# Block 1's attention emitted directly after block 0's, and a first pass of four weight tiles instead of eight

## Chip, cores and metric

The kernel runs on one core of one Trainium2 chip. The metric is the device time of one execution in microseconds (us), the median of several executions. A profile is one execution more, taken with the hardware profiler on; its own time is given beside its span below.

## What is computed

Windowed causal attention over 8 batches, 8 heads, 576 positions and head size 64, and behind it a feed-forward layer with softplus on the 4608 tokens of width 512 (inner width 2048). All is float32.

```python
scores = scale * np.matmul(q, k.transpose(0, 1, 3, 2))
rel = pos[:, None] - pos[None, :]
mask = (rel >= 0) & (rel < window)          # window = 64
scores = np.where(mask, scores, -1000000000.0)
scores = scores - np.max(scores, axis=-1, keepdims=True)
attn = np.exp(scores)
attn = attn / (np.sum(attn, axis=-1, keepdims=True) + 1e-09)
x = np.matmul(attn, v)                      # then (tokens, heads * head size)
...
h = x @ w_in
g = np.maximum(h, 0.0) + np.log1p(np.exp(-np.abs(h)))
return (g @ w_out).astype(np.float32)
```

## The kernel before

The 4608 tokens are cut into 12 blocks of 384. For each block g the kernel runs the attention in four quarters (hp = 0 to 3, two heads each), which leave the attention's output x, transposed, as a high and a low part per quarter. Then come 16 steps, one per slice f of 128 inner columns. The first half of a step (`ffn_up`, L407) is 12 matmuls 128x384 that multiply x with slice f of w_in, three per quarter. Softplus follows on ScalarE (L411 to L413) and VectorE (L415); the result g is split into two parts (L417 on ScalarE, L418 on VectorE). The second half (`ffn_down`, L428) is 9 matmuls 128x512 that add g times slice f of w_out into three banks of the matmul accumulator. At the end of a block's steps the banks are copied out (L447) and stored (L448).

The weights arrive as 64-bit words, and `load_w(f)` makes float32 parts of slice f: a load by SyncE's queue (L168), one operation on ScalarE (L172), three on VectorE (L173 to L175), and for each of the two matrices a cast on ScalarE (L178) and a subtraction on VectorE (L179). For f up to 11 one load of 1024 KB fetches both matrices (tiles raws and ws); for f from 12 on it is two loads of 512 KB (raw and wh). The buffers of raw are two, and the stores of finished blocks use the same two.

Blocks 0 and 1 take a shorter form of the attention (by_pe): scores on TensorE (L260), the masked minimum on VectorE (L271, L277), the exponent on ScalarE (L281), the normalisation on VectorE (L286, L287, L289), transposes on TensorE (L296), copies back (L297), the product with v on TensorE (L353) and the split of x (L358 on ScalarE, L359 on VectorE). From block 2 on the operands are split into parts first (L238, L239, L244, L245), the scores are L264, and the transposes of the probabilities are made by DMA (L313, L318) ahead of the product with v (L382).

Block 0 goes over the weights in two passes. The first pass takes slices 0 to SPLIT-1, and its sums are stored in DRAM (L448, tile part). Then block 1 takes all 16 slices, and then block 0 takes the rest, and its first sums are fetched and added (L442). After that the blocks 2 to 11 follow. So the steps have one running number n: with SPLIT = 8 block 0 has n = 0 to 7, block 1 n = 8 to 23, block 0 again n = 24 to 31.

Each part of the work is an event with a number: `ffn_up` of step n stands at 2n + 0.5, `ffn_down` at 2n + DOWN, `load_w(f)` at CONVERT[f], and quarter hp of the attention of block g < 3 at BASE[g] + PACE[g] * hp plus the stage offsets of STG0 (or STG). The events are sorted and emitted in that order. That order sets priorities only: below PE_ORDERED_FROM = 100 the framework's scheduler orders the instructions of every engine, and from there on it orders all but TensorE. On each engine instructions run in the order that came out.

Of the kernel before, what the change touches and what calls it, by code (L numbers as in the profile page):

```python
# [20 lines left out]
CH = 64  # L21
NCH = TB // CH + 1

SPLIT = 8
DOWN = 5.5
CONVERT = (-95.5, -90.5, -85.5, -80.5, -6, -3, 0, 3, 6, 8, 11, 13, 16, 18, 21, 24)
BASE = (-100, -10, 24)
PACE = (5, 4, 7)
STG0 = (-4.5, 0.5, 1, 2, 3, 4, 7, 8)
STG = (-13, -5.9, -5, 0, 1, 2, 3, 4, 5, 6, 7, 7.1, 12, 14, 16, 17)  # L30
# [9 lines left out]
def window_attention_softplus_ffn(  # L40
# [111 lines left out]
    def load_w(f):  # L152


        if f < NE + 4:
            k = FIRST[f % 4] if f < NE else (4, 6)[f % 2]
            parts = [(spare(k, [P, 2, DM], w_words.dtype, "raws"), spare(k + 1, [P, 2, DM], F32, "ws"), 0, 2)]
        else:
            parts = [
                (  # L160
                    ff.tile([P, 1, DM], w_words.dtype, name="raw"),
                    att.tile([P, 1, DM], F32, name="wh", tag=("v_in", "v12")[m]),
                    m, m + 1,
                )
                for m in range(2)
            ]
        for raw, w, m0, m1 in parts:
            nc.sync.dma_start(raw, w_words[f][:, m0:m1, :])  # L168
            words = raw.bitcast(U32).rearrange("p m (n two) -> p two m n", two=2)
            low, high = words[:, 0, :, :], words[:, 1, :, :]  # L170
            wb = w.bitcast(U32)
            nc.scalar.activation(w, high.bitcast(F32), AF.Abs, scale=REBIAS)  # L172
            nc.vector.tensor_scalar(wb, wb, 3, None, ALU.logical_shift_left)  # L173
            nc.vector.scalar_tensor_tensor(wb, high, 0x80000000, wb, ALU.bitwise_and, ALU.bitwise_or)  # L174
            nc.vector.scalar_tensor_tensor(wb, low, 29, wb, ALU.logical_shift_right, ALU.bitwise_or)  # L175
            for m in range(m0, m1):
                hi, lo = [weight(m, i, f) for i in range(2)]
                nc.scalar.copy(hi, w[:, m - m0, :])  # L178
                nc.vector.tensor_tensor(lo, w[:, m - m0, :], hi.bitcast(F32), ALU.subtract)  # L179
# [273 lines left out]

    passes = [(0, 0, SPLIT), (1, 0, NF), (0, SPLIT, NF)] + [(g, 0, NF) for g in range(2, NB)]
    steps = [(g, f, f == f0, f == f1 - 1) for g, f0, f1 in passes for f in range(f0, f1)]
# [5 lines left out]
    for g in range(NB):  # L461
        for hp in range(NP):
            if g < 3:
                base = BASE[g] + PACE[g] * hp
            else:
# [5 lines left out]
    for n, (g, f, first, last) in enumerate(steps):  # L471
        if f == loaded:
            events.append((CONVERT[f], lambda f=f: load_w(f)))
            loaded += 1
# [54 lines left out]
```

## Time and profile before

| | |
|---|---|
| median of 3 executions | 1032.41 us (1032.14 to 1032.76) |
| profiled execution, its own time | 1035.78 us |
| its span | 1034.0 us |
| mean granted TensorE clock | 0.97 |
| VectorE (DVE) busy | 802.4 us, 78% |
| ScalarE (ACT) busy | 741.9 us, 72% |
| moved by DMA | 119.05 MB, 115 GB/s on average |

In the profile PE is TensorE, PEld its weight loads, DVE VectorE, ACT ScalarE, POOL GpSimd, SP SyncE, which issues the DMAs (SPq). A row of a timeline gives the start and the busy time in us, the engine, line and operation, the tiles, the count, and in brackets the idle time ahead of it with what ended it. Instructions on VectorE and ScalarE overlap a little, so the distance from one start to the next, about 0.1 us less than the busy time, is what one costs in a full queue.

### The profile page before, as it was taken

How to read it: one execution, taken by the hardware profiler on the slowest of the kernel's cores; microseconds unless marked ns; L12 is line 12 of the kernel's file. 1: busy time of each engine (PE TensorE's matmuls, PEld its weight loads, DVE VectorE, ACT ScalarE, POOL GpSimd, SP SyncE). 2: the span in 40 equal slices, each digit the busy share in tenths (PEclk: the TensorE clock that was granted, in tenths of full speed). 3: DMA queues.
4: the chain of work that ended last, by engine and by line, in shares of the span. 5: the costliest groups of instructions: out<-in, count | busy, mean ns of one | idle time of the engine just before them, and what ended most of it. 6: DMA issues, size and time to landing. Idle time of an engine off the chain costs nothing.

```text
span 1034.0 us, 16622 instructions
## 1 busy us (share of the span) xinstructions
PE 982.4 (95%) x5888; PEld 867.2 (84%) x5888; DVE 802.4 (78%) x1817; ACT 741.9 (72%) x1705; POOL 3.9 (0%) x14
## 2 busy tenths in 40 slices
PE   6669579999999999999999999999999999999998
PEld 3458369888888899899988989899899889989997
DVE  6899786587878878878878878887988887974332
ACT  3567477687778778778778778878877877865443
POOL 1000000000000000000000000000000000000000
PEclk9679789999999999999999999999999999999999
DMA  6774353256445546535534634634635645521000
GB/s 189 279 227 137 107 138 83 49 156 150 113 97 122 140 93 119 147 83 119 157 82 114 163 82 113 162 84 112 154 91 104 158 97 103 140 49 31 31 1 31
DMA packets 203155, 119.05 MB, mean 115 GB/s; under 512 B 130880, under 2 KB 195136, under 8 KB 201536
## 3 DMA queue, kind: packets, MB, share of 16 engines
q1 hardware_dynamic: 203072, 118.00, 45.5%
q8 instruction: 46, 0.75, 0.3%
q14 instruction: 37, 0.30, 0.1%
HBM read 76.28 MB, written 10.22 MB: 84 GB/s over the span
## 4 chain that ended last, share of the span: by engine, by line
PE 88%; DMA 4%; DVE 4%; ACT 2%; issue 1%; SPq 0%; ACTq 0%; DVEq 0%
PE ps_h L407 37%; PE ps_o L428 37%; PE ps_a L382 5%; PE ps_a L264 5%; DMA raws<-in_w_words_dram 1%; PE ps_a L260 1%; PE ps_a L353 1%; ACT st L281 1%; DVE ws L175 1%; DMA tr<-nat 1%; DMA part<-raw 0%; DVE w L179 0%; DVE st L271 0%; DMA v_in<-in_v_dram 0%; DVE ws L174 0%
## 5 line engine op out<-in xcount | busy, mean ns | idle before, releaser
L407 PE MATMUL ps_h<-x,w 128*128 128x384 f32 x2304 | 450.5, 343 | 21.5 <-DVE u L415 7.3
L407 PEld LDWEIGHTS ps_h<-x,w 128*128 128x128 f32 x2304 | 407.5, 191 | 37.5 <-ACT w L178 12.3
L428 PE MATMUL ps_o<-w,g 128*128 128x512 f32 x1728 | 438.5, 397 | 0.4 <-DVE g L418 0.4
L428 PEld LDWEIGHTS ps_o<-w,g 128*128 128x128 f32 x1728 | 319.7, 189 | 58.8 <-DVE g L418 0.8
L411 ACT ACTIVATE u<-ps_h 128x384 f32<-128x384 f32 x192 | 94.0, 489 | 135.6 <-PE ps_h L407 133.0
L415 DVE SCALAR_TENSOR_TENSOR u<-ps_h,u 128x384 f32<-128x384 f32 x192 | 106.3, 554 | 73.2 <-ACT u L413 72.0
L281 ACT ACTIVATE st<-st,mn 128x128 f32<-128x128 f32 x288 | 111.9, 390 | 16.3 <-DVE st L277 16.3
L418 DVE TENSOR_TENSOR g<-u,g 128x384 fp32r<-128x384 f32 x192 | 105.7, 551 | 11.0 <-ACT g L417 9.4
L271 DVE CUSTOM_DVE_ANT_0 st<-ps_a,mask 128x192 f32<-128x192 f32 x216 | 69.7, 351 | 51.9 <-PE ps_a L264 50.7
L412 ACT ACTIVATE u<-u 128x384 f32<-128x384 f32 x192 | 100.8, 526 | 3.4
L413 ACT ACTIVATE u<-u 128x384 f32<-128x384 f32 x192 | 100.1, 522 | 4.0
L264 PE MATMUL ps_a<-k,q_hl 128*128 128x192 f32 x480 | 77.1, 284 | 0.9 <-DVE q_hl L239 0.9
L382 PEld LDWEIGHTS <-v 128*128 128x128 bf16 x1088 | 56.1, 98 | 23.5 <-issue 23.1
L382 PE MATMUL ps_a<-tr,v 128*128 128x128 bf16 (+1 forms) x1088 | 70.7, 213 | 1.9 <-DMA tr<-nat 1.9
L264 PEld LDWEIGHTS ps_a<-k,q_hl 128*128 128x128 f32 x480 | 67.3, 194 | 4.8 <-DVE q_hl L239 1.3
L417 ACT CAST g<-u 128x384 fp32r<-128x384 f32 x112 | 56.9, 509 | 13.7 <-DVE u L415 13.0
L312 ACT CAST nat<-st 128x768 bf16<-128x768 f32 x40 | 33.2, 831 | 41.8 <-DVE st L310 41.7
L281 ACT ACTIVATION_READ_ACCUMULATOR st<-st,mn 128x1 f32 x288 | 54.0, 187 | 0.0
L387 ACT COPY xf<-ps_a 64x384 f32<-64x384 f32 x80 | 38.1, 476 | 21.5 <-PE ps_a L382 20.2
L388 DVE TENSOR_TENSOR xf<-ps_a,xf 64x384 f32<-64x384 f32 x80 | 43.8, 548 | 5.0 <-ACT xf L387 3.7
L289 DVE TENSOR_TENSOR st<-st,sm 128x768 f32<-128x768 f32 x48 | 45.9, 957 | 1.4
L331 DVE TENSOR_TENSOR v_in<-v_in,v 128x896 f32<-128x896 f32 x40 | 43.5, 1087 | 3.1 <-ACT v L330 2.9
(80 smaller groups left out, 814.6 us busy)
## 6 DMA issues: line engine op xcount, KB each, us to landing
k_in<-in_kT_dram SPq DMA_DIRECT2D x80, 224.0 KB, 3.9
v_in<-in_v_dram SPq DMA_DIRECT2D x80, 224.0 KB, 3.6
q_in<-in_qT_dram SPq DMA_DIRECT2D x84, 192.0 KB, 4.0
raws<-in_w_words_dram SPq DMA_DIRECT2D x12, 1024.0 KB, 5.6
out_dram<-raw SPq DMA_DIRECT2D x12, 512.0 KB, 2.8
raw<-in_w_words_dram SPq DMA_DIRECT2D x8, 512.0 KB, 4.3
out_dram<-raw SPq DMA_DIRECT2D x12, 256.0 KB, 2.6
v_t<-in_v_dram SPq DMA_DIRECT2D x16, 96.0 KB, 3.6
```

The costliest lines, as they stand in the source:

```text
L264: mm(spv[:, hh, :], q_hl[:, hh, js], part[:, hh, kc], start=(hh == 0 and i == 0), stop=(hh == 1 and i == 1), skip_group_check=True,)
L271: nc.vector.tensor_tensor_reduce(st[:, hh, j, :], spv[:, hh, :], m, QSCALE, 3.0e38, ALU.add, ALU.min, mn[:, hh, j : j + 1])
L281: nc.scalar.activation(sv[:, i, 0:P], sv[:, i, 0:P], AF.Exp, bias=mn[:, hh, j : j + 1], scale=-1.0, accum_out=sm[:, i : i + 1])
L382: mm(av[:, osl], (v13 if s else v12)[:, c, hh, :, :], src, start=(i == 0), stop=(i == len(passes) - 1), skip_group_check=True,)
L407: mm(hv, weight(0, a, f)[:, c * P : (c + 1) * P], x[b][c], start=(i_mm == 0), stop=(i_mm == 3 * NC - 1))
L411: nc.scalar.activation(u, hv, AF.Abs)
L412: nc.scalar.activation(u, u, AF.Exp, scale=-1.0)
L413: nc.scalar.activation(u, u, AF.Ln, bias=1.0)
L415: nc.vector.scalar_tensor_tensor(gf, hv, 0.0, u, ALU.max, ALU.add)
L417: (nc.scalar.copy if g < 2 or f % 2 else nc.vector.tensor_copy)(gt[0], gf)
L418: nc.vector.tensor_tensor(gt[1], gf, gt[0].bitcast(F32), ALU.subtract)
L428: mm(ops[g][j], gt[a][:, js], weight(1, b, f), start=(first and i == 0), stop=(last and i == 2),)
```

## The change

Three of the numbers that place the events change.

```diff
-SPLIT = 8
+SPLIT = 4
 DOWN = 5.5
-CONVERT = (-95.5, -90.5, -85.5, -80.5, -6, -3, 0, 3, 6, 8, 11, 13, 16, 18, 21, 24)
-BASE = (-100, -10, 24)
+CONVERT = (-95.5, -85.5, -72.5, -60.5, -4, -2, 0, 2, 4, 6, 8, 10, 12, 14, 16, 18)
+BASE = (-100, -79, 24)
 PACE = (5, 4, 7)
```

Block 0's first pass now has the steps n = 0 to 3, block 1 has n = 4 to 19, block 0's rest n = 20 to 31. Block 1's attention is emitted from -83.5 on, directly behind block 0's (which ends at -77), instead of from -14.5 on. Slices 1 to 3 are converted later in the emitted order, slices 4 to 15 stand closer together.

What the scheduler makes of it is shown at three places. The first is VectorE behind the end of block 0's first pass, which is the last g1 of that pass (g1_971 before, g1_819 after). Before the change; wh_1043 and wh_1045 are slice 13, pt_623 belongs to the third quarter of block 1's attention and st_659 to its fourth, raw_1099 takes the first sums:

```order
L418 TENSOR_TENSOR g1_971<-u_965,g0_970 128x384
L179 TENSOR_TENSOR w111_1002<-wh_986,w101_1001 128x512
L179 TENSOR_TENSOR w011_993<-wh_1043,w001_992 128x512
L297 COPY pt_623<-ps_a_629 128x384
L173 TENSOR_SCALAR wh_1045<-wh_1045 128x512
L271 ISA st_659,mn_660<-ps_a_662,mask_c_112 128x192
L271 ISA mn_660 128x1
L271 ISA st_659,mn_660<-ps_a_662,mask_c_112 128x192
L271 ISA mn_660 128x1
L447 COPY raw_1099<-ps_o0_716 128x512
L174 SCALAR_TENSOR_TENSOR wh_1045<-raw_1044,wh_1045 128x512
```

After the change; ws_832 is slice 10, ws_790 slice 9, sm_446 belongs to the second quarter of block 1's attention:

```order
L418 TENSOR_TENSOR g1_819<-u_813,g0_818 128x384
L173 TENSOR_SCALAR ws_832<-ws_832 128x1024
L447 COPY raw_922<-ps_o0_777 128x512
L174 SCALAR_TENSOR_TENSOR ws_832<-raws_831,ws_832 128x1024
L447 COPY raw_926<-ps_o2_779 128x512
L286 TENSOR_SCALAR sm_446<-sm_446 128x6
L175 SCALAR_TENSOR_TENSOR ws_832<-raws_831,ws_832 128x1024
L173 TENSOR_SCALAR ws_790<-ws_790 128x1024
L287 RECIPROCAL sm_446<-sm_446 128x6
L174 SCALAR_TENSOR_TENSOR ws_790<-raws_789,ws_790 128x1024
```

The first pass now ends when slices 9 to 15 and more than two quarters of block 1's attention are still to come; before, these were two and a half slices and less than two quarters.

The second place is TensorE at the last quarter of block 1's attention. Before (ps_h_1005 and ps_h_1063 are the steps n = 8 and 9, the first two of block 1):

```order
L296 MATMUL ps_a_747<-ident_115,st_659 128x128 x3
L296 MATMUL ps_a_752<-ident_115,st_659 128x128 x3
L353 MATMUL ps_a_838<-pt_746,v_t_101 64x64 x12
L407 MATMUL ps_h_1005<-x0_3_1_836,w00_85 128x384
L407 MATMUL ps_h_1063<-x0_3_1_836,w00_85 128x384
L407 MATMUL ps_h_1005<-x1_3_1_837,w00_85 128x384
L407 MATMUL ps_h_1005<-x0_3_1_836,w01_86 128x384
L407 MATMUL ps_h_1063<-x1_3_1_837,w00_85 128x384
L407 MATMUL ps_h_1063<-x0_3_1_836,w01_86 128x384
L264 MATMUL ps_a_1192<-k0_1085,q_hl_1060 128x192
```

After (ps_h_842 and ps_h_884 are n = 4 and 5, again the first two of block 1):

```order
L296 MATMUL ps_a_614<-ident_115,st_571 128x128 x3
L296 MATMUL ps_a_619<-ident_115,st_571 128x128 x3
L353 MATMUL ps_a_637<-pt_613,v_t_101 64x64 x12
L407 MATMUL ps_h_842<-x0_3_1_635,w00_85 128x384
L407 MATMUL ps_h_884<-x0_3_1_635,w00_85 128x384
L407 MATMUL ps_h_842<-x1_3_1_636,w00_85 128x384
L407 MATMUL ps_h_842<-x0_3_1_635,w01_86 128x384
L407 MATMUL ps_h_884<-x1_3_1_636,w00_85 128x384
L407 MATMUL ps_h_884<-x0_3_1_635,w01_86 128x384
L264 MATMUL ps_a_1210<-k0_1132,q_hl_1107 128x192
```

The order is the same, but four steps fewer stand ahead of it.

The third place is SyncE's queue from the store of block 0's first sums on. Before:

```order
L448 DMA part_1098<-raw_1099 128x2x512
L214 DMA q_in_884<-in_qT_dram 64x2x384 x2
L168 DMA raw_1128<-in_w_words_dram 128x512
L217 DMA k_in_1037<-in_kT_dram 64x2x448 x2
L448 DMA part_1098<-raw_1103 128x512
L168 DMA raw_1130<-in_w_words_dram 128x512
L168 DMA raw_1199<-in_w_words_dram 128x512
L168 DMA raw_1201<-in_w_words_dram 128x512
```

After:

```order
L448 DMA part_921<-raw_922 128x2x512
L448 DMA part_921<-raw_926 128x512
L168 DMA raw_929<-in_w_words_dram 128x512
L168 DMA raw_931<-in_w_words_dram 128x512
L168 DMA raws_873<-in_w_words_dram 128x1024
L228 DMA v_t_101<-in_v_dram 128x3x128
L228 DMA v_t_101<-in_v_dram 64x3x128 x2
L217 DMA k_in_907<-in_kT_dram 64x2x448 x2
L168 DMA raw_985<-in_w_words_dram 128x512
L168 DMA raw_987<-in_w_words_dram 128x512
L168 DMA raw_1034<-in_w_words_dram 128x512
```

Before, four half slices (14 and 15) follow the store in the two raw buffers; after, all eight (12 to 15) do, and slice 12's two loads, which before stood early in the queue, are among them.

## Prediction

> **What bounds the kernel now.** I read the page first: the engines' shares and the slices of the span.
>
> ```profile
> span 1034.0 us, 16622 instructions
> ...
> PE 982.4 (95%) x5888; PEld 867.2 (84%) x5888; DVE 802.4 (78%) x1817; ACT 741.9 (72%) x1705; POOL 3.9 (0%) x14
> ...
> PE   6669579999999999999999999999999999999998
> ...
> PEclk9679789999999999999999999999999999999999
> ```
>
> TensorE is full from about the seventh slice (26 us each) to the end. So nearly everything that this change can win or lose lies in the first 155 us, and the rest of the kernel only moves earlier or later. What fills TensorE's gaps there is read from the busy time by stretch (columns as named in the first line):
>
> ```profile
> core 0: us, PE busy (x) PEld busy (x) DVE busy (x) ACT busy (x) POOL busy (x), PEclk, DMA share, GB/s
> 20.00:138.71 118.71, 86.33 (x462) 67.69 (x460) 103.47 (x228) 73.76 (x177) 0.00 (x0) 0.78 0.58 187
> 138.71:154.55 15.84, 11.68 (x63) 9.76 (x63) 14.89 (x41) 12.84 (x40) 0.00 (x0) 0.98 0.56 137
> 154.55:233.94 79.39, 79.39 (x464) 70.74 (x464) 56.11 (x123) 59.46 (x134) 0.00 (x0) 0.98 0.40 97
> ```
>
> From 20 to 138.71 us VectorE is busy for 103.47 of 118.71 us and TensorE for 86.33 at a granted clock of 0.78; from 154.55 on TensorE has no gap until 233.94. The cut at 138.71 is the first softplus (L415) of block 1, step n = 8, and 154.55 is the start of the 13th `ffn_up`. So **the start is VectorE's** (conversion of weights, attention of two blocks), and TensorE does steps beside it as far as it has weights and x. The idle 15.24 us of VectorE in the first stretch, by group (count, busy us and mean ns, then idle us and releaser):
>
> ```profile
> L173 DVE TENSOR_SCALAR ws<-ws 128x1024 uint32<-128x1024 uint32 x12 | 8.2, 687 | 4.1 <-ACT ws L172 4.0
> L173 DVE TENSOR_SCALAR wh<-wh 128x512 uint32<-128x512 uint32 x8 | 3.4, 424 | 4.8 <-ACT wh L172 4.7
> L297 DVE COPY pt<-ps_a 128x384 f32<-128x384 f32 x5 | 2.8, 552 | 1.1 <-PE ps_a L296 1.1
> L286 DVE TENSOR_SCALAR sm<-sm 128x6 f32<-128x6 f32 x6 | 1.0, 161 | 4.1 <-ACT st L281 4.1
> ```
>
> 8.9 us wait for loaded weights, 4.1 us for the exponents of an attention quarter.
>
> **The change part by part.** Nothing is added or removed; the total work of every engine stays. A step moved from before block 1 to after it is what counts, because work beside VectorE's stage is covered and work behind it is not. The prices come from TensorE's timeline:
>
> ```profile
> 107.35 2.29 PE L407 MATMUL ps_h<-x,w 128*128 128x384 f32 x6 [3.38 <-DVE u L415]
> 109.44 2.76 PE L428 MATMUL ps_o<-w,g 128*128 128x512 f32 x6
> ...
> 139.31 2.36 PE L407 MATMUL ps_h<-x,w 128*128 128x384 f32 x12 [1.61 <-DVE u L415]
> ...
> 154.55 3.71 PE L407 MATMUL ps_h<-x,w 128*128 128x384 f32 x12 [2.02 <-DVE u L415]
> 158.09 2.24 PE L428 MATMUL ps_o<-w,g 128*128 128x512 f32 x9
> 160.17 2.27 PE L407 MATMUL ps_h<-x,w 128*128 128x384 f32 x12
> 162.28 2.25 PE L428 MATMUL ps_o<-w,g 128*128 128x512 f32 x9
> ...
> 231.23 0.59 PE L264 MATMUL ps_a<-k,q_hl 128*128 128x192 f32 x4
> 231.65 2.30 PE L407 MATMUL ps_h<-x,w 128*128 128x384 f32 x12
> 235.82 0.68 PE L382 MATMUL ps_a<-tr,v 128*128 128x64 bf16 x7 [1.88 <-DMA tr<-nat]
> 236.31 2.91 PE L428 MATMUL ps_o<-w,g 128*128 128x512 f32 x6
> 239.01 0.78 PE L264 MATMUL ps_a<-k,q_hl 128*128 128x192 f32 x4
> ```
>
> An `ffn_up` costs 162.28 - 160.17 = 2.11 us, an `ffn_down` 160.17 - 158.09 = 2.08, four scores of block 2 231.65 - 231.23 = 0.42.
>
> *VectorE's work ahead of block 1's first softplus.* Its row in VectorE's order has 271 instructions ahead of it before (20 to 138.71 shows x228, the first 20 us the rest) and 262 after. By kind the difference is: 4 of L415 and 4 of L418 fewer (the four steps), 2 of L271 with their 2 accumulator reads fewer, and one each of L174, L175 and L179 for a half slice more. The price of one is the distance to the next start:
>
> ```profile
> 135.46 0.68 DVE L179 TENSOR_TENSOR w<-wh,w 128x512 fp32r<-128x512 f32 x1
> 136.06 0.68 DVE L174 SCALAR_TENSOR_TENSOR wh<-raw,wh 128x512 uint32<-128x512 uint32 x1
> 136.66 0.35 DVE L271 CUSTOM_DVE_ANT_0 st<-ps_a,mask 128x192 f32<-128x192 f32 x1
> 136.94 0.08 DVE L271 DVE_READ_ACCUMULATOR2_ANT mn<- 128x1 f32 x1
> ...
> 138.71 0.55 DVE L415 SCALAR_TENSOR_TENSOR u<-ps_h,u 128x384 f32<-128x384 f32 x1
> 139.18 0.34 DVE L271 CUSTOM_DVE_ANT_0 st<-ps_a,mask 128x192 f32<-128x192 f32 x1
> ```
>
> That is 8 x 0.47 = 3.8 less, 2 x 0.28 = 0.6 less, 3 x 0.60 = 1.8 more: **2.5 us less** of 103.5. All slices but parts of the last, and all of block 1's attention, stand ahead of that softplus as before. Emitting block 1's attention at -83.5 does not bring its last x forward on VectorE: it is row 252 instead of row 256.
>
> *VectorE's idle time ahead of it.* Two causes shrink. Slice 12's two early half loads no longer stand ahead of slice 0, so slice 4's buffer comes free sooner, and most of the 4.1 us ahead of L173 (ws) should go: I take 2.5 to 3. And fewer steps stand in ScalarE's queue ahead of the exponents. One grows: slices 12 to 15 all pass the two raw buffers behind the store of block 0's first sums, where before it was 14 and 15. The chain of waits shows what one such passage is:
>
> ```profile
> 97.59 4.40 DMA k_in<-in_kT_dram
> 102.07 0.95 ACT k L244
> ...
> 120.92 4.99 DMA part<-raw
> 125.92 3.31 DMA raw<-in_w_words_dram
> 129.31 0.66 ACT wh L172
> ```
>
> Store 4.99, load 3.31, ScalarE 0.66. Of that VectorE has other work for a part, and two pairs more may bring 1 to 3 us more idle. The wait for k_in (4.40, then L244 0.95 ahead of the exponents on ScalarE) stays: k_in_907 still stands behind v_t_101 in SyncE's queue. From the order and these durations I get 3 us less idle in sum. The bounds: at best all four groups above go (14.1 us less), at worst two pairs more each pay store-free passages of 3.31 that nothing covers (6.6 us more). I take 3 less because the big items of both kinds stay. So block 1's first softplus comes at 138.71 - 2.5 - 3 = **133.2 us**, and TensorE's next `ffn_up` 0.6 us behind it, as 139.31 is behind 138.71: 133.8.
>
> *TensorE from there to the 13th `ffn_up`.* At that point both orders have 12 `ffn_up`, 10 `ffn_down` and 32 scores of block 2 behind them. Before, 2, 2 and 20 of these lie between 139.31 and 154.55: 4.2 + 4.2 + 5 x 0.42 = 10.5 us of work in 15.24, so 4.7 us of waiting and of lower clock. After, it is 6, 6 and 20: 12.7 + 12.5 + 2.1 = 27.3. The waits come from VectorE and ScalarE, which then do block 2's attention (VectorE 14.89 of 15.84 us busy). The same work now has four steps more to lie beside, and the conversions end earlier; I take half of the waits, 2.4, with 1 to 6 as bounds. That gives 133.8 + 27.3 + 2.4 = 163.5 against 154.55: **+9.0 us**.
>
> The lower clock after a wait is in these rows: 6 `ffn_up` matmuls behind the gap of 3.38 us took 109.44 - 107.35 = 2.09 us, twice 2.11 / 2. [...]
>
> *Behind it.* Before, the 13th `ffn_up` starts after a gap and takes 158.09 - 154.55 = 3.54 instead of 2.11; after, TensorE comes to it out of a full stretch: -1.4. The stall at 233.94 (1.88 us for the transposed probabilities, then six matmuls in 239.01 - 236.31 = 2.70 instead of 2.08 x 6 / 9 = 1.39) costs 3.2. There SyncE's queue holds block 1's output store and block 2's transposes close together; in the changed order the store stands four steps earlier and the last transposes do not follow it. I take -2, between 0 and -3.2.
>
> **Sum:** 9.0 - 1.4 - 2 = +5.6 us on the profiled execution's 1035.78, so 1041.4. The median before is 3.37 us under that execution; on it the forecast is 1032.41 + 5.6 = **1038.0 us**.
>
> **The rivals.**
>
> *The full price (slower still).* VectorE's idle time does not shrink: the four pairs through two raw buffers, behind k_in and v_t loads in one queue, take what slice 4 gives back. Then the first softplus is at 136.2 to 139, and if nothing comes back at the stall either, the four steps cost 4 x 4.19 = 16.8 less 2.5: +14.3, so 1046.7. For it: the idle group of wh is the largest of the four (4.8), and it has the same number of halves. Against it: most of slice 4's wait has a cause that goes. [...]
>
> *Faster: the waits of the start collapse.* Block 1's loads and scores stand early, so no quarter waits for k, v or exponents, and VectorE runs without a gap from 25 us on. The price is at most 14.1 us of idle instead of 3, so 11.1 us better: 1038.0 - 11.1 = 1026.9. It decides from a first softplus of block 1 before about 127.5 us (133.2 - 5.6). For it: 4.1 us of the idle are ahead of L286, which earlier scores can cover. Against it: the row of the last x moved by four places only, and the weight waits depend on buffers, not on the emitted place.
>
> *No change.* The scheduler's order undoes the move and what is left cancels: idle shrinks by 7 to 10 us, half of the way to the rival above. 1032.4, within 2 us.
>
> **How the numbers follow.** Slower by 2 to 11 us as worked out: 0.58. The full price, beyond that: 0.15. No change: 0.12. Faster: 0.15. A measurement of this kernel tells about 0.2% (2.1 us) from none. So slower 0.73, same 0.12, faster 0.15. The range reaches down by two thirds of what the idle could still give (about -4) and up to most of the full price (+13): 1028.5 to 1045.5.
>
> **What would show it.** In the changed profile the fifth L415, block 1's first, starts at about 133 us, with some 12 us of VectorE idle between 20 us and it; the 13th `ffn_up` starts at about 163.5; TensorE's idle time up to 240 us grows by about 6 us; no stall for tr above 1 us around 235 us. The forecast is wrong if VectorE's idle time falls by over 8 us (faster), or if TensorE waits for softplus again and again between 134 and 164 us (slower still).

## The result and the profile after

The changed kernel takes **1047.39 us** (median of 4 runs, 1045.73 to 1048.7) beside 1032.59 us of the kernel before (4 runs, 1032.14 to 1034.97): a ratio of 1.0138, 95% interval 1.0114 to 1.0162. It is slower, as forecast, but by 14.8 us instead of 5.6; the forecast was 1038.0 us and its range ended at 1045.5. The profiled execution took 1048.7 us; its page begins with

```profile
span 1046.9 us, 16627 instructions
...
PE 979.0 (94%) x5888; PEld 864.1 (83%) x5888; DVE 802.6 (77%) x1817; ACT 741.8 (71%) x1705; POOL 4.0 (0%) x14
...
PE   6664599989999999999999999999999999999998
PEclk9877699999999999999999999999999999999999
```

The busy sums have hardly moved. The slices show two places: the fourth and fifth (78 to 131 us) have 4 and 5 tenths of TensorE where before there were 9 and 5, and the ninth (209 to 236 us) has 8. The same two places in the windows (columns as in the prediction: length, then busy time of PE, PEld, DVE, ACT and POOL, clock, DMA share, GB/s):

```profile
20.00:132.13 112.13, 66.55 (x364) 49.74 (x363) 100.31 (x214) 66.81 (x163) 0.00 (x0) 0.74 0.61 199
...
164.50:200.00 35.50, 35.50 (x185) 31.79 (x183) 10.50 (x23) 17.97 (x35) 0.00 (x0) 1.00 0.00 1
200.00:240.00 40.00, 36.36 (x246) 31.25 (x245) 36.44 (x82) 33.83 (x84) 0.00 (x0) 1.00 0.80 186
```

The first row ends at block 1's first softplus: VectorE is idle for 112.13 - 100.31 = 11.8 us ahead of it. The second and third are new. From 164.5 to 200 us TensorE runs without a gap, VectorE does 10.50 us of work, and the DMA share is 0.00; from 200 to 240 VectorE is full (36.44 of 40) and TensorE waits. The same stretch in the kernel before, whose TensorE is some ten us further on in its work by then, had VectorE at 18.49 and a DMA share of 0.23:

```profile
164.50:200.00 35.50, 35.50 (x201) 31.69 (x199) 18.49 (x35) 23.66 (x52) 0.00 (x0) 1.00 0.23 58
200.00:240.00 40.00, 38.12 (x249) 33.70 (x248) 33.22 (x77) 32.13 (x75) 0.00 (x0) 0.96 0.61 146
```

TensorE's rows of the changed kernel with a wait, from the 13th `ffn_up` (164.48 us, before 154.55) to 300 us:

```profile
164.48 2.33 PE L407 MATMUL ps_h<-x,w 128*128 128x384 f32 x12
...
220.84 2.38 PE L407 MATMUL ps_h<-x,w 128*128 128x384 f32 x12 [0.62 <-DVE u L415]
229.90 1.65 PE L428 MATMUL ps_o<-w,g 128*128 128x512 f32 x6 [0.40 <-ACT g L417]
234.89 2.38 PE L407 MATMUL ps_h<-x,w 128*128 128x384 f32 x12 [1.97 <-DVE u L415]
237.92 1.66 PE L428 MATMUL ps_o<-w,g 128*128 128x512 f32 x6 [0.65 <-ACT g L417]
248.11 2.38 PE L407 MATMUL ps_h<-x,w 128*128 128x384 f32 x12 [1.25 <-DVE u L415]
263.29 0.96 PE L428 MATMUL ps_o<-w,g 128*128 128x512 f32 x3 [0.23 <-DVE g L418]
265.56 2.35 PE L407 MATMUL ps_h<-x,w 128*128 128x384 f32 x12 [1.30 <-DVE u L415]
269.85 0.51 PE L382 MATMUL ps_a<-tr,v 128*128 128x64 bf16 x7 [0.56 <-DMA tr<-nat]
```

They sum to 7.0 us, and 6.4 of them wait for softplus, on VectorE and ScalarE. So the 12.9 us between the two spans are 9.9 us up to the 13th `ffn_up` and 3.0 us behind it (1046.9 - 164.48 = 882.4 against 1034.0 - 154.55 = 879.4). In that last part TensorE's idle time grew by 5.1 us (11.5 against 6.4) and its busy time fell by 2.1.

### The profile page after: what moved, and what is told of

The parts are those of the page before. It is cut to its first block, busy times and chain, and to the rows that moved or that the text cites. A ratio compares the mean times of both kernels' runs of the same rounds, so it can differ in the third digit from the quotient of the medians.

```text
span 1046.9 us, 16627 instructions
## 1 busy us (share of the span) xinstructions
PE 979.0 (94%) x5888; PEld 864.1 (83%) x5888; DVE 802.6 (77%) x1817; ACT 741.8 (71%) x1705; POOL 4.0 (0%) x14
## 3 DMA queue, kind: packets, MB, share of 16 engines
q1 hardware_dynamic: 203072, 118.00, 45.2%
## 4 chain that ended last, share of the span: by engine, by line
PE 82%; DMA 7%; ACT 5%; DVE 4%; issue 1%; SPq 1%; ACTq 0%; DVEq 0%
PE ps_h L407 36%; PE ps_o L428 35%; PE ps_a L382 5%; PE ps_a L264 5%; DMA raws<-in_w_words_dram 3%; ACT st L281 2%; PE ps_a L260 1%; DMA v_in<-in_v_dram 1%; DMA k_in<-in_kT_dram 1%; DMA tr<-nat 1%; DMA raw<-in_w_words_dram 1%; DVE st L271 1%; PE ps_a L353 0%; ACT u L411 0%; DVE w L179 0%
## 5 line engine op out<-in xcount | busy, mean ns | idle before, releaser
L407 PE MATMUL ps_h<-x,w 128*128 128x384 f32 x2304 | 449.4, 343 | 27.5 <-DVE u L415 16.8
L415 DVE SCALAR_TENSOR_TENSOR u<-ps_h,u 128x384 f32<-128x384 f32 x192 | 106.2, 554 | 92.9 <-ACT u L413 91.4
L281 ACT ACTIVATION_READ_ACCUMULATOR st<-st,mn 128x1 f32 x288 | 54.3, 188 | 0.0
```

Source lines behind the costliest of these rows:

```text
L281: nc.scalar.activation(sv[:, i, 0:P], sv[:, i, 0:P], AF.Exp, bias=mn[:, hh, j : j + 1], scale=-1.0, accum_out=sm[:, i : i + 1])
L407: mm(hv, weight(0, a, f)[:, c * P : (c + 1) * P], x[b][c], start=(i_mm == 0), stop=(i_mm == 3 * NC - 1))
L415: nc.vector.scalar_tensor_tensor(gf, hv, 0.0, u, ALU.max, ALU.add)
```

## The experiments

One table for all runs, for reference. "Steps ahead" is SPLIT, the steps of block 0 that stand ahead of block 1; the third column is the start of block 1's first L415; the next two are TensorE's idle time (window length less busy time). Spans and windows are of the one profiled execution, which can lie off its kernel's median: before is profiled at 1035.78 us (median 1032.59), product_earlier at 1049.69 (1046.09), block2_at_12 at 1040.39 (1038.01), split6 at 1032.61 (1034.05). So differences of 3 us between spans, or between starts in two profiles, are not read as effects by themselves. The ratio is to runs of the kernel before on the same chip.

| kernel | steps ahead | block 1's first L415 | idle 0 to 200 | idle 200 to 300 | span | ratio (95%) |
|---|---|---|---|---|---|---|
| before | 8 | 138.7 | 45.2 | 1.9 | 1034.0 | |
| changed | 4 | 132.1 | 56.4 | 7.0 | 1046.9 | 1.0138 (1.0114 to 1.0162) |
| split4_alone | 4 | 132.6 | 54.3 | 7.1 | 1047.4 | 1.0149 (1.0115 to 1.0183) |
| order_alone | 8 | 131.5 | 38.0 | 0.1 | 1021.8 | 0.9885 (0.9855 to 0.9915) |
| first_four | 8 | 132.0 | 44.9 | 5.7 | 1033.8 | 1.0021 (1.0004 to 1.0038) |
| rest_of_slices | 8 | 133.3 | 39.1 | 1.7 | 1023.6 | 0.9944 (0.9924 to 0.9965) |
| split6 | 6 | 131.1 | 50.1 | 0.3 | 1030.8 | 1.0017 (0.9997 to 1.0037) |
| split10 | 10 | 131.7 | 35.1 | 0.0 | 1016.1 | 0.9839 (0.9805 to 0.9873) |
| split11 | 11 | 132.4 | 32.2 | 5.3 | 1017.0 | 0.9874 (0.9842 to 0.9905) |
| split12 | 12 | 135.0 | 33.0 | 5.9 | 1020.7 | 0.9921 (0.9898 to 0.9944) |
| block2_at_18 | 4 | 129.2 | 54.6 | 6.2 | 1045.9 | 1.0138 (1.0108 to 1.0168) |
| block2_at_12 | 4 | 131.8 | 54.9 | 0.0 | 1038.6 | 1.0039 (1.0022 to 1.0055) |
| qk_on_gpsimd | 4 | 137.3 | 61.1 | 2.2 | 1059.9 | 1.0297 (1.0266 to 1.0327) |
| qk_on_gpsimd_before | 8 | 135.3 | 42.2 | 10.1 | 1036.6 | 1.0101 (1.0066 to 1.0135) |
| product_earlier | 4 | 135.8 | 54.3 | 5.3 | 1047.9 | 1.0146 (1.0114 to 1.0177) |
| product_far_earlier | 4 | 133.2 | 55.4 | 0.9 | 1041.0 | 1.0096 (1.0068 to 1.0124) |

### Taking the change apart

The emitted place of block 1's attention could be settled without a run. With four steps ahead and the new places of the slices, emitting it at -18 instead of -79 gives the same program, instruction for instruction; so do -10 and -79 with eight steps ahead. With these values the order that comes out hangs on the first pass and on the places of the slices alone. These two were run apart. **split4_alone** is the kernel before with

```diff
-SPLIT = 8
+SPLIT = 4
-BASE = (-100, -10, 24)
+BASE = (-100, -18, 24)
```

(the -18 is needed because with -10 block 1's steps would be emitted ahead of its x).

> The kernel before with SPLIT = 4 and nothing else of the change; block 1's attention is emitted at -18 instead of -10, since with SPLIT = 4 its steps begin 8 earlier. Theory (the four steps moved behind block 1's attention are the cause, and the emitted place of that attention is none): as the changed kernel, 1045 to 1049 us, ratio 1.012 to 1.016. Rival (the new emitted order of attention and conversions costs the time): 1036 us or less.

Measured: 1049.74 us, ratio 1.0149: the theory's by the ratio, a little above its range in us, and the intervals of this and of the changed kernel overlap. The program differs from the changed one in eight rows of VectorE, two of ScalarE and two of SyncE, where the load of half a k and that of half a slice change places. With four steps ahead the new places of the slices do next to nothing. **order_alone** is the changed kernel with eight steps ahead again:

```diff
-SPLIT = 4
+SPLIT = 8
```

> The changed kernel with SPLIT = 8: the new places of block 1's attention and of the conversions without the split. Theory: the steps stand beside VectorE's work again, so 1030 to 1036 us, ratio 0.997 to 1.003. Rival (the emitted order is the cause): 1042 us or more.

Measured: 1021.98 us, ratio 0.9885. Neither theory had this: the new places of the slices make the kernel **11 us faster** as long as eight steps stand ahead, and taking four of these away then costs 25 us. So the change is a gain and a larger loss, not one loss of 14.8. Where the 25 us are is read from two windows that meet at block 1's first softplus, first of order_alone, then of the changed kernel:

```profile
0.00:131.50 131.50, 96.12 (x492) 71.93 (x492) 110.75 (x261) 79.04 (x200) 3.94 (x14) 0.83 0.56 186
131.50:1021.80 890.30, 883.00 (x5396) 791.55 (x5396) 690.62 (x1557) 662.23 (x1506) 0.00 (x0) 1.00 0.45 106
```

```profile
0.00:132.13 132.13, 78.09 (x408) 56.37 (x408) 111.26 (x261) 73.46 (x189) 3.96 (x14) 0.77 0.61 194
132.13:1046.90 914.77, 900.88 (x5480) 807.77 (x5480) 691.39 (x1557) 668.34 (x1517) 0.00 (x0) 1.00 0.43 102
```

The first stretch is as long in both, with the same 261 instructions on VectorE; TensorE has 408 matmuls in it instead of 492. The 84 missing ones (4 x 21) come behind, for 900.88 - 883.00 = 17.9 us, and TensorE's idle time behind the softplus grows from 7.3 to 13.9 us. Together with 0.6 us at the front that is the whole difference of the spans: 0.6 + 17.9 + 6.6 = 25.1.

### Which of the new places gain

**first_four** and **rest_of_slices** are the kernel before with one part each of the new places:

```diff
-CONVERT = (-95.5, -90.5, -85.5, -80.5, -6, ...
+CONVERT = (-95.5, -85.5, -72.5, -60.5, -6, ...
```

> The kernel before with the new places of slices 0 to 3 alone (-95.5, -85.5, -72.5, -60.5). Theory (the gain of the new places is made here: with slices 1 to 3 behind block 0's attention, VectorE's order ahead of block 1's first softplus is seven rows shorter and the 3.22 us wait for slice 13's half, which stood behind the store of the first sums, goes): 1022 to 1026, block 1's first softplus at 131 to 135 us. Rival (the gain is made by the closer places of slices 4 to 15): 1033, within 2 us, first softplus at 138 to 139.

```diff
-CONVERT = (..., -80.5, -6, -3, 0, 3, 6, 8, 11, 13, 16, 18, 21, 24)
+CONVERT = (..., -80.5, -4, -2, 0, 2, 4, 6, 8, 10, 12, 14, 16, 18)
```

> The kernel before with the new places of slices 4 to 15 alone. Theory (these places hardly matter; VectorE's order ahead of block 1's first softplus is two rows longer than before): 1033 to 1035, first softplus of block 1 at 138 to 140 us. Rival (these places make the gain): 1022 to 1026, first softplus at 131 to 135.

Measured: 1035.44 us (ratio 1.0021) and 1027.05 us (0.9944). My theory fell in both, and the rivals' times were missed as well, by 0.4 and 1.1 us. The first half does bring block 1's first softplus to 132.0 us, 6.7 earlier, but the whole gain is lost again behind it, 3.8 us of it as further waits from 200 to 300 us (5.7 against 1.9); the second half brings it to 133.3 and keeps part of it. The halves don't add up to the 1.15% of order_alone; what they do only together, the runs don't show. Either half is enough for the front, and in every kernel but the one before, product_earlier (135.8) and the two with loads issued by GpSimd, that softplus stands between 129 and 135 us, whatever number of steps is ahead. The kernel before is 4 us beyond that: of its 138.7 us, 3.22 are one wait for slice 14's second half (not slice 13's, as the text on record has it), whose load stands behind the second store of the first sums, the passage of 4.99, 3.31 and 0.66 us in the prediction,

```profile
130.01 0.43 DVE L173 TENSOR_SCALAR wh<-wh 128x512 uint32<-128x512 uint32 x1 [3.22 <-ACT wh L172]
```

and in the changed kernel the longest wait for such a half (wh) ahead of that softplus is 1.03 us. The two latest starts with loads on SyncE, 138.7 and 135.8, are both from executions over 3 us above their medians, so a part of these 4 us may belong to the execution and not to the order; one profile of each can't tell.

### The number of steps ahead

The changed kernel with `SPLIT = 6`, `10`, `11` and `12` (one line each, as in order_alone).

> The changed numbers with a first pass of six steps. Theory (a step moved from before block 1 to behind it costs its whole TensorE time, 4.2 us, and the further 7 us of the four-step version come from block 2's attention standing still and then bunching, which happens only when the rest of block 1 is short of conversions): with six steps block 2's second transposes stand after steps 15 to 17 as with eight, so no bunching: 1022 + 2 x 4.2 = 1030.4, between 1028 and 1033, and TensorE is busy for over 99 of the 100 us from 200 to 300. Rival (the cost is one and the same slope from eight to four, 25.4 / 4 = 6.4 us a step): 1034.7, and TensorE waits 3 to 4 us from 200 to 300.

> The changed numbers with a first pass of ten steps. Theory (TensorE has gaps to spare ahead of block 1, and every step set there is taken from behind): VectorE has two softplus steps more ahead of block 1, 2 x 0.94 = 1.9 us, and TensorE saves 2 x 4.2: 1022 - 8.4 + 1.9 = 1015.5, between 1012 and 1019. Rival (the weights of slices 8 and 9 are finished too late to be used ahead of block 1, so that TensorE has no gap left that fits): 1022, within 3 us; or the ninth and tenth steps hold up block 1's x in the queues and it is 1025 to 1030.

> The changed numbers with a first pass of twelve steps. Theory (ahead of block 1's first softplus, at 131 to 133 us in every version but before, TensorE has idle time of 30 us with ten steps, so two steps more still fit): 1017.1 - 8.4 + 2 for VectorE and some of the idle that cannot be used, between 1008 and 1014. Rival (the weights of slices 10 and 11 and their softplus now stand in front of block 1's attention on VectorE, whose order ahead of block 1's first softplus grows from 268 to 276 rows): block 1's first softplus at 136 to 140 and 1016 to 1021.

> The changed numbers with a first pass of eleven steps, between ten (1017.1) and twelve (1022.4, with 5.9 us of TensorE waits from 200 to 300). By the front alone a step more is worth up to 4.2 us: 1013. By the waits behind (the product of block 2's second quarter stands behind steps 23 and 24 as with ten): they decide, and with the same order as ten it is 1013 to 1016; if the waits of twelve are there too, 1018 to 1021.

Measured: split6 1034.05 us (span 1030.8), split10 1017.1, split11 1018.83, split12 1022.39. From eight to six steps the span grows by 9.0 us, 2 x 4.19 and 0.6, with 99.67 of 100 us busy from 200 to 300: the theory's mechanism. By the medians it is 12 us, and 1034.05 lies above the theory's 1033 and near the rival's 1034.7, whose 3 to 4 us of waits are not there (0.3). The 3 us between the two readings are those of the profiled executions: order_alone's is 1.6 us above its median, split6's 1.4 below. From eight to ten 5.7 us of span come where 6.5 were expected, and 1017.1 is in the theory's range. Beyond ten the front goes on giving little (idle 32.2 and 33.0 us up to 200 against 35.1) and the stretch from 200 to 300 takes it back: 5.3 and 5.9 us of waits. With eleven the time is in the range given for that case (1018 to 1021). With twelve the softplus of block 1 is at 135.0 us, short of the rival's 136, and the time is above both theories because neither had the later waits. **split10 has the lowest time of this study**, 1.6% below the kernel before (0.9839, 0.9805 to 0.9873); its interval touches those of eight and eleven steps, so that ten is better than these is not shown beyond the noise.

### What makes TensorE wait between 200 and 300 us

Between 164 and 200 us the changed kernel's TensorE has only steps, and the products of block 2's first quarter stand between them one by one:

```profile
164.33 0.34 PE L382 MATMUL ps_a<-tr,v 128*128 128x128 bf16 x3
172.92 0.23 PE L382 MATMUL ps_a<-tr,v 128*128 128x128 bf16 x1
181.40 0.23 PE L382 MATMUL ps_a<-tr,v 128*128 128x128 bf16 x1
189.88 0.20 PE L382 MATMUL ps_a<-tr,v 128*128 128x64 bf16 x1
200.91 0.85 PE L382 MATMUL ps_a<-tr,v 128*128 128x64 bf16 x14
210.94 0.85 PE L382 MATMUL ps_a<-tr,v 128*128 128x64 bf16 x14
```

The first four are 0.20 to 0.34 us of work each, 8.5 us apart, that is, two steps. Only behind block 1's last step, at 200.91, does the rest follow, and then quickly. Steps are counted from one here, as in the texts on record (step 23 is n = 22): by TensorE's order the products of block 2's quarters 2 to 4 and of block 3's first stand behind steps 23, 25, 27 and 29, where before they were spread over the steps 24 to 35. Four experiments ask whether this standing still and bunching is the cause. Two give block 2's attention an earlier place (changed kernel, `BASE[2]` 18 and 12 instead of 24):

> The changed kernel with the attention of block 2 emitted from 18 instead of 24 on, three steps earlier. Theory: TensorE's 7 us of idle between 200 and 275 us come from block 2's attention, which stands still while VectorE is idle between 164 and 200 us and is then bunched; half to all of it goes: 1040 to 1044 us. Rival (those waits are the price of the softplus chain itself, or the start alone decides): 1046 to 1049 us.

> The same with 12 instead of 24. Theory: the waits between 200 and 275 us go, 1039 to 1042 us, and what is left over the kernel before is the price of the four steps, 7 to 10 us. Rival (the start alone decides): 1046 to 1049 us. If block 2's attention then stands in the way of block 1's steps, above 1049 us.

Measured: 1047.93 and 1038.01 us. Six places do next to nothing, as the rival said (idle from 200 to 300 us 6.2): the second quarter moves up to the steps 20 and 21, but block 3's first is still through by step 29. Twelve places take every wait away (0.0) and 9.4 us off the time, and there the last of these products reaches to step 35. What is left is the price of the four steps: the span is 16.8 us above order_alone's (1038.6 against 1021.8; 16.0 by the medians), and four steps are 4 x 4.19 = 16.8. (The text on record reckoned it from the kernel before, which lacks the gain of the new places.) The window and the rows of block2_at_12 at the same place:

```profile
200.00:300.00 100.00, 100.00 (x605) 89.36 (x604) 72.78 (x161) 74.20 (x168) 0.00 (x0) 1.00 0.43 106
```

```profile
164.05 0.34 PE L382 MATMUL ps_a<-tr,v 128*128 128x128 bf16 x3
172.64 0.32 PE L382 MATMUL ps_a<-tr,v 128*128 128x128 bf16 x3
175.41 0.85 PE L382 MATMUL ps_a<-tr,v 128*128 128x64 bf16 x14
185.44 0.51 PE L382 MATMUL ps_a<-tr,v 128*128 128x64 bf16 x7
```

The second quarter is in its products by 185 us, beside block 1's steps. Two more move the products alone, in the changed kernel's loop over the stages of block 2 (in the second with -14):

```diff
             for at in STG if g >= 2 else STG0:
+                at = at - 4.5 if g == 2 and at > 7.5 else at
```

> The changed kernel with one edit: the four stages of block 2's product with v (at 12, 14, 16 and 17) are emitted 4.5 places earlier. In the changed kernel the 28 matmuls of that product for block 2's first quarter begin behind step 10, then stand singly between the steps 12 to 19 in TensorE's order, and end behind step 21, and everything of the later quarters waits for them. With this edit they stand together behind steps 10 and 11, and the product of the second quarter ends behind step 22 instead of 23. Theory (this spreading is what makes block 2's attention stand still and then bunch, and the bunching is what costs the waits of TensorE between 220 and 270 us): VectorE busy for over 15 of the 40 us from 160 to 200, TensorE for 96 or more of the 100 us from 200 to 300, 1041 to 1045. Rival (the second quarter still comes behind step 20, and only that counts): the waits stay, 1046 to 1049.

> As before, but 14 places earlier: the product of block 2's first quarter now ends behind step 17, those of the second stand behind 19 and 20, of the third behind 23 and 24, of the fourth behind 26 and 27, each some three steps ahead of the changed kernel except the last. Theory (the further the quarters are apart from block 1's end, the fewer waits): TensorE busy for 98 or more of the 100 us from 200 to 300, 1039 to 1043. Rival (the order of block 2's own quarters does not matter, the waits come from the missing four steps themselves): 1046 to 1049.

Measured: 1046.09 and 1041.88 us. product_earlier is the rival's by its time: the first quarter's products do stand together, but the second's still begin only at 205.49 us, and there are 5.3 us of waits. They are not those of the changed kernel, though: 2.1 us wait for softplus where it was 6.4, the rest stands ahead of scores and products:

```profile
229.72 0.69 PE L264 MATMUL ps_a<-k,q_hl 128*128 128x192 f32 x4 [1.91 <-DVE mn L271]
231.27 0.84 PE L264 MATMUL ps_a<-k,q_hl 128*128 128x192 f32 x4 [0.86 <-DVE xf L388]
234.24 4.21 PE L407 MATMUL ps_h<-x,w 128*128 128x384 f32 x12 [2.13 <-DVE u L415]
```

product_far_earlier is the theory's: 99.06 of 100 us busy, and 5.5 us off the median (4.3 by the ratios, whose intervals still overlap a little):

```profile
160.00:200.00 40.00, 40.00 (x235) 35.79 (x234) 22.39 (x53) 25.96 (x56) 0.00 (x0) 1.00 0.23 53
200.00:300.00 100.00, 99.06 (x618) 88.69 (x617) 82.29 (x184) 79.88 (x185) 0.00 (x0) 1.00 0.53 127
```

Two edits that bring block 2's second quarter through by step 20 and leave block 3's first until step 35 remove the waits (0.0 and 0.9 us) with four steps ahead, so the four missing steps don't make them by themselves; they come from where block 2's attention lies. Putting the first quarter's products together alone isn't enough. A rule by which one could tell the waits from the order was not found: split11, split12 and first_four have 5.3 to 5.9 us of waits, and not all of one kind. Of split11's, 0.6 us wait for softplus; 4.6 stand ahead of products and wait for transposes or for VectorE's masked minimum. One regularity of the programs fits the bunching: from block 2's second quarter to block 3's second, none of the five kernels with less than 1 us of waits has a quarter whose 28 products all stand behind one step of TensorE's order, and every kernel with more than 5 us except product_earlier has one or more (the changed kernel four). That was seen afterwards and no run tests it.

A third way failed. SyncE's queue in the changed kernel has one long wait between 140 and 280 us:

```profile
SPq L217 <- DVE g L418: 48.8, 1, 48.8
SPq L324 <- DVE u L415: 7.2, 2, 6.8
```

(line, released by: us in total, times, longest.) The load of block 3's first k waits 48.8 us for its only buffer, and the transposes of block 2's second quarter stand behind it. **qk_on_gpsimd** takes these loads out of the queue, in the changed kernel and in the one before:

```diff
-                nc.sync.dma_start(
+                nc.gpsimd.dma_start(
                     q_in[half, :, :], qT[c0 : c0 + P, ts].rearrange("(h d) t -> d h t", h=2)
...
-                nc.sync.dma_start(
+                nc.gpsimd.dma_start(
                     k_in[half, :, :], kT[c0 : c0 + P, ks].rearrange("(h d) t -> d h t", h=2)
```

> The changed kernel with one edit: from block 2 on the loads of q and k are issued by GpSimd instead of SyncE. Theory (the 5 to 7 us of TensorE waits from 200 to 300 us come from SyncE's queue: the load of block 3's first k waits 48.8 us for its only buffer, which VectorE frees behind step 19, and the transposes of block 2's second quarter stand behind that load): without that load in the queue block 2's second transposes come after steps 13 and 14, VectorE is busy for over 20 of the 40 us from 160 to 200, TensorE for over 99 of the 100 from 200 to 300, and the time is 1047.4 - 6 = 1041, between 1038 and 1044. Rival (block 2's attention is too late whatever the queue does, because four steps fewer of block 1 lie beside it): the waits stay and it is 1046 to 1049. A gain of more than 10 us would mean that the queue also held up the start.

> The kernel before with the same edit as a control. Theory: its longest wait of SyncE for a k buffer is 13.4 us and TensorE has only 1.9 us of gaps from 154.55 to 300, so at most 2 to 3 us are to be had: 1030 to 1034. Rival (the edit helps or harms by itself, through the start): over 5 us to either side.

Measured: 1060.29 and 1039.97 us, 13 (16 by the ratios) and 10 us slower than without the edit, the first beyond theory and rival, the second as its rival had it. In the stretch in question the theory holds for the most part (VectorE 31.18 of 40 us from 160 to 200 against 12.84, TensorE 97.80 of 100 from 200 to 300 against 93.03, where over 99 was expected), but block 1's first softplus comes 5.2 us later, and the waits return elsewhere:

```profile
296.95 1.63 PE L428 MATMUL ps_o<-w,g 128*128 128x512 f32 x6 [1.00 <-ACT g L417]
...
305.25 1.44 PE L382 MATMUL ps_a<-tr,v 128*128 128x64 bf16 x14 [3.97 <-DMA tr<-nat]
317.20 1.67 PE L428 MATMUL ps_o<-w,g 128*128 128x512 f32 x6 [1.13 <-ACT g L417]
322.81 0.51 PE L382 MATMUL ps_a<-tr,v 128*128 128x64 bf16 x7 [1.85 <-DMA tr<-nat]
```

The edit changes the whole order, and the control is harmed as well (10.1 us of waits from 200 to 300), so it doesn't tell whether SyncE's wait is a cause or follows from TensorE's order. That stays open.

## Why the prediction was right and wrong

*What bounds the kernel* was right in its kind and too narrow: the time is decided by TensorE's gaps, but in the first 300 us, where the prediction put nearly everything into the first 155. Over the kernels with loads on SyncE, the span less the idle time of the first 300 us is 979 to 988 us, while the spans run from 1016 to 1048.

*VectorE ahead of block 1's first softplus* came out right in its sum and wrong in its parts. The softplus was forecast at 133.2 us and came at 132.13, with 11.8 us of VectorE idle where 12 was forecast and 3.2 us of work less where 2.5 was. But by group:

```profile
L173 DVE TENSOR_SCALAR ws<-ws 128x1024 uint32<-128x1024 uint32 x12 | 8.2, 682 | 6.2 <-ACT ws L172 6.1
L173 DVE TENSOR_SCALAR wh<-wh 128x512 uint32<-128x512 uint32 x8 | 3.4, 423 | 1.4 <-ACT wh L172 1.3
L286 DVE TENSOR_SCALAR sm<-sm 128x6 f32<-128x6 f32 x6 | 1.0, 165 | 3.0 <-ACT st L281 3.0
```

The wait for whole slices (ws) was to lose 2.5 to 3 us and grew from 4.1 to 6.2 (one wait of 3.71 us went, three of 2.0 us came, at 29.42, 52.79 and 87.32 us); the wait for half slices (wh) was to grow by 1 to 3 and fell from 4.8 to 1.4. Two errors of opposite sign: that the idle time came out was luck.

*From there to the 13th `ffn_up`* came out near: 163.5 forecast, 164.48 measured, +9.9 instead of +9.0 us. The work counted was the right one (6, 6 and 20), but the stretch took 31.7 us where 29.7 was forecast: 4.4 us above the counted 27.3 instead of 2.4, within the bounds of 1 to 6. Half of this excess was hidden by the softplus that came 1.1 us early.

**The step that failed is "Behind it".** I credited 1.4 us for the 13th `ffn_up`, which ran at a granted clock of 0.59 before (154.55 to 158.09 us), and 2 us for the stall at 233.94, so -3.4 in sum; the runs have +3.0. The 13th `ffn_up` does run at a granted clock of 1.00 (2.33 us in place of 3.71), so the first credit is there. The second isn't. I looked only at SyncE's order around that one stall and put new waits at nothing, without asking what block 2's attention would then lie beside: the stall of 1.88 us did go, and eight new waits of 7.0 us in sum came. That they come from where block 2's attention lies is shown (block2_at_12 takes them all away); that the packing of its quarters into the steps 23 to 29 is the way, is my reading. This step is 6.4 of the 7.3 us by which the span's growth was off (12.9 against 5.6). Another 1.9 us lie between the profiled executions and the medians (12.9 against 14.8).

*The rivals.* The number that came is the full price's (1046.7 forecast, 1047.39 measured), but not by its way: it wanted the softplus at 136 to 139 us and no gain at the front. The front gained 6.6 us, and the loss came behind; that its number was met was luck. The four steps that no longer stand beside VectorE's stage cost 17.9 us of TensorE's time behind it. That no change comes of it because the order undoes the move is true of one part only, the emitted place of block 1's attention.

*What I didn't see at all* is that the places of the slices are worth 11 us by themselves with eight steps ahead, because I priced them only together with the shorter first pass.

## What to carry to other kernels

A step moved out of a stretch that another engine bounds cost its whole time here (17.9 us of TensorE's time for four steps of 4.19 us), and so the number of such steps is worth a sweep: here ten had the lowest time, and more gave nothing, because the front gave at most 3 us more and the next stage began to wait. When work moves ahead of or behind a stage, ask of the next block beside which steps its own work will stand; a stretch in which the helping engines rest while the main one is full (VectorE 10.50 of 35.50 us here) can mean that they will be late afterwards. It is no sure sign: split11 has waits of 5.3 us behind a stretch with VectorE busy for 29.72 of 40 us. And change numbers of an order one at a time: a gain of 11 us and a loss of 25 stood in this one diff.

## What the hardware showed that was not expected

How long the matmuls behind a wait take doesn't follow from the length of that wait. In the changed kernel 12 matmuls of `ffn_up` took 2.38 us behind a wait of 1.97 us, at a granted clock of 1.00 (234.89 to 237.27 us), about as long as without one (2.33 at 164.48 us, also at 1.00); in first_four they took 3.67 behind a shorter wait of 1.82 us:

```profile
257.78 3.67 PE L407 MATMUL ps_h<-x,w 128*128 128x384 f32 x12 [1.82 <-DVE u L415]
```

Over the window from 200 to 300 us, 7.0 us of waits left the granted clock of the changed kernel at 1.00, and 5.7 us left that of first_four at 0.97 (the changed kernel's row, then first_four's):

```profile
200.00:300.00 100.00, 93.03 (x604) 81.42 (x603) 87.92 (x193) 81.93 (x195) 0.00 (x0) 1.00 0.64 151
```

```profile
200.00:300.00 100.00, 94.32 (x573) 82.65 (x572) 79.78 (x175) 74.85 (x174) 0.00 (x0) 0.97 0.53 129
```

What decides the clock, no run here shows.

Loads issued by GpSimd in qk_on_gpsimd landed in the median as fast as SyncE's in the changed kernel (k_in between 100 and 320 us: 3.8 us in both), each with 0.6 us of GpSimd's time, but the slowest took 7.3 us against 4.9.
